# Dealing one block of the output projection unevenly over the DMA engines

## The chip, the cores and the metric

One core of a Trainium2 chip. The metric is device time in microseconds (us) of one execution of the kernel. Engines are named as in the profile: PE (TensorE matmuls), PEld (its weight loads), DVE (VectorE), ACT (ScalarE), POOL (GpSimd), SP (SyncE, whose queue issues nearly all transfers here). The core has 16 DMA engines, on which all transfers run.

## The reference, cut to what matters

```python
xn = layernorm(x)                              # x: [2, 1, 512]
q  = (xn @ wq)                                 # 32 heads of 128
k, v = caches[:, :, -4096:, :]                 # 8 kv heads, the last 4096 of 32768 positions
o  = softmax(q @ k.T / sqrt(128)) @ v          # each kv head serves 4 heads
s  = o.reshape(2, 1, 4096) @ wo                # wo: [4096, 512]
z  = gelu(xn @ w_in); z1, z2 = halves of z     # w_in: [512, 1792]
g  = silu((z1 * (w_sp * layernorm(z2) + b_sp)) @ w_out)
return x + s * g
```

All of it is fp32, two batch rows and one position. Nearly every byte that is read (wq, w_in, w_out, wo and the window of both caches, 89.4 MB together) is used once.

## The kernel before, in words

Everything large comes through one queue: SP issues the transfers in program order, `w_in`, `w_out`, `wq` in two halves, then one 4 MB load of k or v for each of the 8 kv heads (a "unit"), and `wo` last. All 4 MB loads, the halves of wq, `w_in` and the two parts of `wo` share a ring of four SBUF slots (`slot`), so that SP waits at most issues for the unit that last used the slot. SP also reuses eight landing semaphores in turn: an issue that gets a semaphore waits until the transfer that had it before has landed.

For each unit DVE turns k in four pieces (`turn`, tile `kt`), PE makes scores (`s`), DVE and ACT make probabilities (`sm`, `p`), PE and DVE bring them into shape (`pp`, `pT`), and PE multiplies them with v (`values`, tile `acc`). `collect` and `spread` gather the heads of a set of units into `oT`, the weights for the output projection. There are three sets (`SETS`): units 0 to 3 with 16 blocks of `wo`, units 4 and 5 with 8, units 6 and 7 with 8. A block is 128 rows of `wo`, one on each partition, and within a set row 16p + j (or 8p + j) belongs to partition p of block j.

The last part of the program multiplies `oT` with the blocks of `wo` as they land. The blocks of the sets 0 and 1 are added up in the PSUM tile `part`, each step on one of four column strips of PE; `wo_early` emits one landed piece of these. Then ACT copies `part` to `parts`, PE folds the four strips into `so` with `rowm`, and the blocks of set 2 are added to `so` directly, in pieces of 4, 2, 1 and 1 blocks, in the order in which they land. DVE multiplies `so` with the gate and adds x (`res`), and ACT issues the store.

`wo` is loaded in eight transfers, in this order: blocks 0 to 7 and 8 to 15 of set 0 (2 MB each), blocks 0 to 3 and 4 to 7 of set 1, and 4, 2, 1 and 1 blocks of set 2:

```python
for j, n in (((0, 8), (8, 8)), ((0, 4), (4, 4)), ((0, 4), (4, 2), (6, 1), (7, 1)))[i]:
    sp.dma_start(t[:, a : a + n, :], wo_s[i][:, j : j + n, :])
    blocks.append((t[:, a : a + n, :], sets[f"oT{i}"][1], j))
```

The helper `InOrder` records every operation of PE, DVE, ACT and SP, so that in the profile they all stand at its line 37; tiles tell them apart.

Of the kernel before, what the change touches and what calls it, by code (L numbers as in the profile page):

```python
# [9 lines left out]
F32 = mybir.dt.float32  # L10
# [4 lines left out]
P = 128  # L15
# [6 lines left out]
def free_ap(t, offset, dims):  # L22

    return bass.AP(tensor=t.tensor, offset=t.offset + offset, ap=[list(t.ap[0])] + [list(d) for d in dims])
# [18 lines left out]
def kernel(  # L43
# [13 lines left out]
    nc = tc.nc  # L57
    pe, dve, act, sp = (InOrder(tc, e) for e in (nc.tensor, nc.vector, nc.scalar, nc.sync))
    B, _, D = x.shape
    _, HKV, SK, _ = k_cache.shape  # L60
# [20 lines left out]
    cst = ctx.enter_context(tc.tile_pool(name="cst", bufs=1))  # L81
# [3 lines left out]
    def slot(name, *shape):  # L85
        return ring.tile([P, *shape], F32, tag="slot", name=name)

    def bank(name, *shape):
        return ps.tile([P, *shape], F32, tag="kt", name=name, bufs=3)
# [11 lines left out]
    for a in range(0, KT, 2):  # L101
        t = slot(f"wq{a}", 2, HQ * DH)
# [1 line left out]
        wqt += [t[:, 0], t[:, 1]]  # L104

    wb1 = cst.tile([1, 2], F32, tag="wb1", name="wb1")
    act.dma_start(wb1[:, 0:1], bass.AP(tensor=w_sp.tensor, offset=w_sp.offset, ap=[[1, 1], [1, 1]]))
    act.dma_start(wb1[:, 1:2], bass.AP(tensor=b_sp.tensor, offset=b_sp.offset, ap=[[1, 1], [1, 1]]))
    x4 = low.tile([P, DC], F32, tag="x4", name="x4")
    nc.gpsimd.memset(x4, 0.0)  # L110
    by_group = [[DC, G], [D, B], [1, DC]]
# [14 lines left out]
    def turn(p, c):  # L126
        t = sb.tile([P, CT, G, 32], F32, tag="kt", name=f"kt{p.n}_{c}", bufs=4)
        dve.transpose(t.rearrange("p t j y -> p (t j y)"), p.k[:, CT * c : CT * c + CT, :].rearrange("p t d -> p (t d)"))
        p.kt.append(t)

    units = []
    for n in range(HKV):
        p = Unit()
        p.n, p.kt, p.s = n, [], None
        units.append(p)
    AHEAD = 2
# [8 lines left out]
    ident = cst.tile([P, P], F32, tag="ident", name="ident")  # L145
# [8 lines left out]
    hT = low.tile([P, FT, 32], F32, tag="hT", name="hT")  # L154
    nc.gpsimd.memset(hT, 0.0)

    rowm = cst.tile([P, 32], F32, tag="rowm", name="rowm")
    dve.tensor_reduce(rowm, ident.rearrange("p (g c) -> p c g", g=G), axis=AX.X, op=ALU.add)

    def rsqrt(dst, a, tag):  # L160
        t = cst.tile(list(a.shape), F32, tag="rt" + tag, name="rt" + tag)
        act.activation(t, a, AF.Ln)
        act.activation(dst, t, AF.Exp, scale=-0.5)
        dve.tensor_mul(t, dst, dst)
        dve.tensor_mul(t, t, a)
        dve.tensor_scalar(t, t, -0.5, 1.5, op0=ALU.mult, op1=ALU.add)
        dve.tensor_mul(dst, dst, t)


    st = cst.tile([B, nc.vector.BN_STATS_DIM], F32, tag="st", name="st")  # L170
    dve.bn_stats(st, xs)
    mv = cst.tile([B, nc.vector.BN_AGGR_DIM], F32, tag="mv", name="mv")
    dve.bn_aggr(mv, st)
    va = cst.tile([B, 1], F32, tag="va", name="va")
    dve.tensor_scalar_add(va, mv[:, 1:2], EPS)
    rs = cst.tile([B, 1], F32, tag="rs", name="rs")
    rsqrt(rs, va, "x")
    xn = sb.tile([B, D], F32, tag="o", name="xn", bufs=1)
    dve.tensor_scalar(xn, xs, mv[:, 0:1], rs, op0=ALU.subtract, op1=ALU.mult)
    pt = bank("xnT_ps", KT, B)  # L180
# [26 lines left out]
    def place(n, nx):  # L207
        t = cst.tile([P, nx, n, REP, G, nx], F32, tag=f"place{n}", name=f"place{n}")
        nc.gpsimd.memset(t, 0.0)
        for x in range(nx):  # L210
            dve.tensor_add(
                t[:, x, :, :, :, x], *(free_ap(ident, REP * b, [[E, n], [1, REP], [32, G]]) for b in range(B))
            )
        return t
# [6 lines left out]
    for k in range(KT):  # L221
        for n in range(G):
# [3 lines left out]
                start=(k == 0), stop=(k == KT - 1),  # L226
# [14 lines left out]
    def queries(k):  # L241
        for r in range(NR):
            for g in range(G):
                c = (r * G + g) * 512
                pe.matmul(
                    pq[r][32 * g : 32 * g + 32, :], xnT[:, k, :], wqt[k][:, c : c + 512],
                    start=(k == 0), stop=(k == KT - 1),
                )
# [34 lines left out]
    dve.tensor_mul(hT[:, :, 0 : 16 * B : 16], z1, z2)  # L283
    queries(2)
    place4 = place(4, 2)
    place2 = place(2, 4)
    py = bank("ys", D)
    for j in range(FT):
# [17 lines left out]
    for r in range(NR):  # L306
        src = pq[r].rearrange("p (i d) -> p i d", i=REP)
# [5 lines left out]
    for r in range(NR):  # L313
        pt = bank(f"qT_ps{r}", REP, G, 32)
# [4 lines left out]
    for j in range(G):  # L319
        pe.matmul(  # L320
            pw[:, j, :], selj[:, j].rearrange("p g c -> p (g c)"), qT.rearrange("p r g b i -> p (r g b i)"),
            start=True, stop=True,
# [10 lines left out]
    sets = {}  # L333
    for i, (kv, n, nj) in enumerate(SETS):
        o1 = cst.tile([P, B, 32], F32, tag=f"o1_{i}", name=f"o1_{i}")
        lt = cst.tile([P, CH], F32, tag=f"lt_{i}", name=f"lt_{i}")
        nc.gpsimd.memset(lt, 1.0)
        oT = cst.tile([P, nj, 32], F32, tag=f"oT_{i}", name=f"oT_{i}")
# [5 lines left out]
    def scores(p, *chunks):  # L344
        if p.s is None:
            p.s = ps.tile([P, 512], F32, tag="s", name=f"s{p.n}", bufs=2)
        for j in range(G):
            for c in chunks:
                pe.matmul(
                    p.s[32 * c : 32 * c + 32, :], qw[:, p.n, j].rearrange("p g e -> p (g e)"), p.kt[c][:, :, j, :],  # L350
                    start=(j == 0), stop=(j == G - 1),
                )
# [93 lines left out]
    def spread(i):  # L446
        o1, oT, nj = sets[f"oT{i}"]
        t = {8: place2, 16: place4}[nj]
        nx = 32 // nj
        pt = bank(f"oT_ps{i}", B, nj)  # L450
        for x in range(nx):
            pe.matmul(
                pt, t[:, x].rearrange("p n h g x -> p (n h g x)"), o1[:, :, nj * x : nj * x + nj],
                start=(x == 0), stop=(x == nx - 1),
            )
        dve.tensor_copy(oT[:, :, 0 : 16 * B : 16], pt.rearrange("p b j -> p j b"))

    ends = {kv + n - 1: i for i, (kv, n, nj) in enumerate(SETS)}
    def gathered(p):
        if p is not None:  # L460
            collect(p)

    def spread_after(p):
        if p is not None and p.n in ends:
            spread(ends[p.n])

    def probabilities(p, between):
        row_max(p)
        share_max(p)
        between(0)  # L470
        bias(p)
        probs(p)
        swapped(p)
        between(1)
        probs_t(p)

    def product(p):
        if p is not None:
            values(p)
            evacuate(p)  # L480

    old = None
    for prev, cur in zip([None] + units, units):
        gathered(old)
        if prev is not None:
            probabilities(prev, lambda c: turn(cur, c))
        turn(cur, 2)
        spread_after(old)
        turn(cur, 3)
        old = prev if cur.n < HKV - AHEAD else units[-3] if cur.n == HKV - 1 else None  # L490
        product(old)
        scores(cur, 0, 1, 2, 3)


    wo_s = []
# [3 lines left out]
    blocks = []  # L499
    for first, of in ((0, (0,)), (1, (1, 2))):  # L500
        t = slot(f"wo{first}", 16, D)
        a = 0
        for i in of:
            nj = SETS[i][2]
            for j, n in (((0, 8), (8, 8)), ((0, 4), (4, 4)), ((0, 4), (4, 2), (6, 1), (7, 1)))[i]:
                sp.dma_start(t[:, a : a + n, :], wo_s[i][:, j : j + n, :])
                blocks.append((t[:, a : a + n, :], sets[f"oT{i}"][1], j))
                a += n
    EARLY = 24
    done = 0  # L510

    def wo_early(n):
        nonlocal done
        t, oT, j = blocks[n]
        for a in range(t.shape[1]):
            g = done % G
            pe.matmul(
                part[32 * g : 32 * g + 32, :], oT[:, j + a, :], t[:, a, :], start=(done < G), stop=(done >= EARLY - G)
            )
            done += 1  # L520
# [9 lines left out]
    wo_early(0)  # L530
    gathered(units[-1])
    spread_after(units[-1])
    for n in range(1, 4):
        wo_early(n)
    parts = sb.tile([P, D], F32, tag="o", name="parts", bufs=1)
    act.activation(parts, part, AF.Copy)
    so = bank("so", DC)
    for g in range(G):
        pe.matmul(so[32 * g : 32 * g + 32, :], rowm, parts[:, g * DC : (g + 1) * DC], start=True, stop=False)
    for n in range(4, len(blocks)):  # L540
        t, oT, j = blocks[n]
        for a in range(t.shape[1]):
            for g in range(G):
                pe.matmul(
                    so[32 * g : 32 * g + 32, :], oT[:, j + a, :], t[:, a, g * DC : (g + 1) * DC],
                    start=False, stop=(j + a == oT.shape[1] - 1),
                )
# [32 lines left out]
```

## Time and profile before

| what | us |
|---|---|
| time, median of 3 runs | 217.88 (217.22 to 217.9) |
| the profiled execution's own time | 217.06 |
| its span in the trace | 215.3 |
| the last piece of wo has landed, in the span | 211.47 |

| engine | busy us | share of the span |
|---|---|---|
| PE | 139.3 | 65% |
| PEld | 44.0 | 20% |
| DVE | 104.8 | 49% |
| ACT | 24.0 | 11% |
| POOL | 4.0 | 2% |

The profiled execution's time is 1.76 us more than its span, which is what lies around the program. The DMA engines moved 89.54 MB in the span, 416 GB/s on average. The page's row of 40 slices shows them at nine tenths or more from the second slice to the last but one.

### The profile page before, as it was taken

The numbers are of one execution on the slowest core, as the hardware profiler recorded it, in microseconds if no ns is written. First come the engines' busy times: TensorE is split into PE (matmuls) and PEld (weight loads), VectorE is DVE, ScalarE is ACT, GpSimd is POOL, SyncE is SP. The second block draws the span as 40 slices with busy tenths as digits, with TensorE's granted clock in tenths as the row PEclk, the third lists the DMA queues.
The fourth block names the chain that finished last, engine by engine and source line by source line (L and its number), as shares of the span: only waits on it lengthen the run. The fifth ranks groups of instructions, "written<-read, shape, count | busy, mean of one in ns | idle before, by whom it ended". The sixth has DMA issues, their size and how long they took to land.

```text
span 215.3 us, 2106 instructions
## 1 busy us (share of the span) xinstructions
PE 139.3 (65%) x862; PEld 44.0 (20%) x862; DVE 104.8 (49%) x161; ACT 24.0 (11%) x60; POOL 4.0 (2%) x20
## 2 busy tenths in 40 slices
PE   0174195827756973982595298089669299969773
PEld 0120021213111211220121022033111022332321
DVE  2604014159658559439506921983693883511201
ACT  5002103110001101011020002102010102021010
POOL 7000000000000000000000000000000000000000
PEclk9999557995596796697579669757967959988789
DMA  7999999999999999999999999999999999999990
GB/s 256 427 438 451 426 438 438 406 457 414 457 408 444 423 438 432 426 451 420 451 405 451 420 444 426 426 451 417 444 414 451 426 440 417 432 417 425 414 386 27
DMA packets 4093, 89.54 MB, mean 416 GB/s; under 512 B 486, under 2 KB 498, under 8 KB 884
## 3 DMA queue, kind: packets, MB, share of 16 engines
q1 hardware_dynamic: 4032, 89.39, 96.8%
q8 instruction: 7, 0.11, 0.2%
q14 instruction: 2, 0.02, 0.0%
q10 hardware_dynamic: 20, 0.01, 0.0%
q0 software_dynamic: 32, 0.00, 0.0%
HBM read 89.40 MB, written 0.00 MB: 415 GB/s over the span
## 4 chain that ended last, share of the span: by engine, by line
DMA 72%; PE 14%; DVE 11%; SPq 1%; ACT 1%; issue 1%; ACTq 0%; DVEq 0%
DMA v<-in_A_v_cache_dram 42%; DMA k<-in_A_k_cache_dram 20%; DMA wo<-in_A_wo_dram 9%; DVE kt L37 8%; PE acc L37 8%; PE s L37 4%; PE pp L37 2%; SPq L37 1%; ACT p L37 1%; DVE pT L37 1%; DVE sm L37 1%; DVE qw L37 1%; DVE res L37 0%; PE so L37 0%; DVE mg L37 0%
## 5 line engine op out<-in xcount | busy, mean ns | idle before, releaser
L37 DVE STREAM_TRANSPOSE kt<-k 128x2048 f32<-128x2048 f32 x32 | 72.5, 2285 | 2.2 <-DMA k<-in_A_k_cache_dram 2.2
L37 PE MATMUL acc<-v,pT 128*32 128x512 f32 x256 | 42.5, 822 | 12.5 <-DMA v<-in_A_v_cache_dram 11.7
L37 PE MATMUL s<-kt,qw 128*32 128x512 f32 x256 | 38.0, 637 | 3.5 <-DVE kt L37 2.9
L37 PE MATMUL pp<-p,swap 128*128 128x512 f32 x16 | 12.5, 871 | 21.2 <-ACT p L37 21.2
L37 DVE CUSTOM_DVE_ANT_1 sm<-s,own 128x512 f32<-128x512 f32 x8 | 5.5, 692 | 34.4 <-PE s L37 34.3
L37 PEld LDWEIGHTS acc<-v,pT 128*32 128x32 f32 x256 | 11.1, 155 | 43.2 <-issue 40.0
L37 PE MATMUL q_ps<-wq,xnT 128*32 128x512 f32 x64 | 11.4, 852 | 10.1 <-DMA wq<-in_A_wq_dram 10.1
L37 ACT ACTIVATE o<-acc,diag 128x128 f32<-128x128 f32 x30 | 8.7, 369 | 72.9 <-PE acc L37 72.5
L37 PEld LDWEIGHTS s<-kt,qw 128*32 128x32 f32 x256 | 9.1, 115 | 30.5 <-issue 19.9
L37 ACT ACTIVATE p<-sm,nb 128x512 f32<-128x512 f32 x8 | 5.8, 724 | 66.5 <-DVE nb L37 66.5
L37 PE MATMUL z<-win,xnT 128*32 128x448 f32 x32 | 6.1, 939 | 4.5 <-DMA win<-in_B_w_in_dram 4.5
L37 DVE STREAM_TRANSPOSE pT<-pp 128x512 f32<-128x512 f32 x8 | 5.7, 715 | 5.6 <-PE pp L37 5.5
L37 PE MATMUL col<-o,selw 128*32 128x128 f32 (+1 forms) x28 | 7.8, 468 | 0.0
L37 DVE TENSOR_TENSOR lsum<-pl,diag 128x4 f32<-128x4 f32 x3 | 0.5, 161 | 14.8 <-PE pl L37 14.8
L37 PEld LDWEIGHTS pp<-p,swap 128*128 128x128 f32 x16 | 3.0, 234 | 22.0 <-ACT p L37 22.0
L37 PE MATMUL part<-wo,oT 128*32 128x512 f32 x48 | 7.4, 751 | 0.1
L37 PE MATMUL mo<-mg,same 128*128 128x16 f32 x16 | 3.2, 273 | 5.8 <-DVE mg L37 5.3
L37 ACT ACT_TABLE_LOAD x4 | 5.1, 1283 | 1.9 <-issue 1.9
L37 DVE STREAM_TRANSPOSE zt<-z 128x448 f32<-128x448 f32 x1 | 1.0, 980 | 8.9 <-ACT z L37 8.9
L37 PEld LDWEIGHTS q_ps<-wq,xnT 128*32 128x32 f32 x64 | 2.2, 142 | 14.7 <-DMA wq<-in_A_wq_dram 10.3
L37 PE MATMUL xnT_ps<-ident,xn 2*128 2x2 f32 x4 | 0.6, 252 | 6.9 <-DVE xn L37 6.9
L37 DVE TENSOR_TENSOR res<-so,gate 128x128 f32<-128x128 f32 x1 | 0.3, 292 | 9.6 <-PE so L37 9.6
(110 smaller groups left out, 66.3 us busy)
## 6 DMA issues: line engine op xcount, KB each, us to landing
k<-in_A_k_cache_dram SPq DMA_DIRECT2D x8, 4096.0 KB, 23.9
v<-in_A_v_cache_dram SPq DMA_DIRECT2D x8, 4096.0 KB, 31.4
wq<-in_A_wq_dram SPq DMA_DIRECT2D x2, 4096.0 KB, 28.8
wo<-in_A_wo_dram SPq DMA_DIRECT2D x2, 2048.0 KB
win<-in_B_w_in_dram SPq DMA_DIRECT2D x1, 3584.0 KB, 11.2
wo<-in_A_wo_dram SPq DMA_DIRECT2D x3, 1024.0 KB, 23.9
wout<-in_B_w_out_dram SPq DMA_DIRECT2D x1, 1792.0 KB, 15.1
wo<-in_A_wo_dram SPq DMA_DIRECT2D x1, 512.0 KB, 28.0
```

What stands on the lines that cost most here:

```text
L37: return self.tc.keep_in_program_order(call(*args, **kwargs))
```

## The change

The 16th block (block 15) of set 0 no longer comes with the blocks 8 to 14. Its 128 rows come in two transfers of their own:

- 80 rows go to partitions 0 to 79. The source is given in two dimensions, 10 by 8: place 8a + b takes row a + 10b.
- 48 rows go to partitions 16 to 63 of a new tile `wob`, whose partitions 0 to 15 are zero. The source is 8 by 6: place 6a + b takes row 80 + a + 8b.

Rows of block 15 thereby sit on other partitions than their weights in `oT`. So two matrices of zeros and ones (`perm`, written once by POOL and DVE) and a new function `deal` bring the weights of block 15 into the same order (`oTx`): two small matmuls and two small copies, in the iteration of unit 6. In the last part the block is two steps in place of one, of 80 and 64 rows, so `part` has 25 steps (`EARLY`).

Beside that, the two loads of single numbers (`w_sp`, `b_sp`) are issued by POOL in place of ACT, and four small tiles of the first layernorm share one.

```diff
-    act.dma_start(wb1[:, 0:1], ...w_sp...)
-    act.dma_start(wb1[:, 1:2], ...b_sp...)
+    nc.gpsimd.dma_start(wb1[:, 0:1], ...w_sp...)
+    nc.gpsimd.dma_start(wb1[:, 1:2], ...b_sp...)
...
+    NA, NBK = 80, 64
+    MA, MB = 10, 8
+    perm = cst.tile([P, NA + NBK], F32, tag="perm", name="perm")
+    nc.gpsimd.memset(perm, 0.0)
+    oTx = cst.tile([P, 2, 32], F32, tag="oTx", name="oTx")
+    nc.gpsimd.memset(oTx, 0.0)
+    wob = cst.tile([P, D], F32, tag="wob", name="wob")
+    nc.gpsimd.memset(wob[0:NBK, :], 0.0)
+    NX = P - NA
+    X0 = NBK - NX
...
+    dve.tensor_copy(
+        perm[:, 0:NA].rearrange("p (e i) -> p e i", e=MA), free_ap(ident, 0, [[1, MA], [MA, NA // MA]])
+    )
+    dve.tensor_copy(
+        perm[:, NA + X0 :].rearrange("p (e i) -> p e i", e=MB), free_ap(ident, NA, [[1, MB], [MB, NX // MB]])
+    )
...
+    def deal():
+        o1, oT, nj = sets["oT0"]
+        pt = bank("oTx_ps", 2, B)
+        for i, rows in ((0, slice(0, NA)), (1, slice(NA, NA + NBK))):
+            n = rows.stop - rows.start
+            pe.matmul(pt[0:n, i, :], perm[:, rows], oT[:, nj - 1, 0 : 16 * B : 16], start=True, stop=True)
+        for i, n in ((0, NA), (1, NBK)):
+            dve.tensor_copy(oTx[0:n, i, 0 : 16 * B : 16], pt[0:n, i, :])
...
         spread_after(old)
+        if cur.n == HKV - AHEAD:
+            deal()
         turn(cur, 3)
...
-            for j, n in (((0, 8), (8, 8)), ((0, 4), (4, 4)), ((0, 4), (4, 2), (6, 1), (7, 1)))[i]:
+            for j, n in (((0, 8), (8, 7)), ((0, 4), (4, 4)), ((0, 4), (4, 2), (6, 1), (7, 1)))[i]:
...
+            if i == 0:
+                for dst, p0, k, n in ((t[0:NA, a, :], 0, MA, NA // MA), (wob[X0:NBK, :], NA, MB, NX // MB)):
+                    src = wo_s[0][p0 : p0 + 1, nj - 1, :]
+                    row = nj * D
+                    sp.dma_start(
+                        dst, bass.AP(tensor=src.tensor, offset=src.offset, ap=[[row, k], [row * k, n], [1, D]])
+                    )
+                blocks.append((t[0:NA, a : a + 1, :], oTx[0:NA], 0))
+                blocks.append((wob[0:NBK, :].rearrange("p (a d) -> p a d", a=1), oTx[0:NBK], 1))
-    EARLY = 24
+    EARLY = 25
...
-    for n in range(1, 4):
+    for n in range(1, 6):
         wo_early(n)
...
-    for n in range(4, len(blocks)):
+    for n in range(6, len(blocks)):
```

On SP, at the end of its program, before (`wo_802` holds set 0, `wo_805` the sets 1 and 2; the sizes are partitions by elements, `DMAHW` are the landing semaphores):

```order
L37 DMA wo_802<-in_A_wo_dram 128x4096 [waits DMAHW3_49,DVE_49]
L37 DMA wo_802<-in_A_wo_dram 128x4096
L37 DMA wo_805<-in_A_wo_dram 128x2048 [waits DMAHW4_49,PE_49]
L37 DMA wo_805<-in_A_wo_dram 128x2048 x2
L37 DMA wo_805<-in_A_wo_dram 128x1024
L37 DMA wo_805<-in_A_wo_dram 128x512 [waits DMAHW5_49]
L37 DMA wo_805<-in_A_wo_dram 128x512 [waits DMAHW6_49]
```

The same place with the change (`wo_812` and `wob` hold set 0, `wo_817` the sets 1 and 2):

```order
L37 DMA wo_812<-in_A_wo_dram 128x4096 [waits DMAHW1_49,DVE_49]
L37 DMA wo_812<-in_A_wo_dram 128x3584
L37 DMA wo_812<-in_A_wo_dram 80x1x512
L37 DMA wob<-in_A_wo_dram 48x1x512 [waits Pool_49]
L37 DMA wo_817<-in_A_wo_dram 128x2048 [waits DMAHW2_49,PE_49]
L37 DMA wo_817<-in_A_wo_dram 128x2048
L37 DMA wo_817<-in_A_wo_dram 128x2048 [waits DMAHW3_49]
L37 DMA wo_817<-in_A_wo_dram 128x1024 [waits DMAHW4_49]
L37 DMA wo_817<-in_A_wo_dram 128x512 [waits DMAHW5_49]
L37 DMA wo_817<-in_A_wo_dram 128x512 [waits DMAHW6_49]
```

Two transfers stand between the second piece of set 0 and set 1. The turn of the eight semaphores has moved: the last two issues had waited for the loads of v of the units 6 and 7, and now wait for the first two pieces of `wo` itself, while the two issues ahead of them wait for those v loads.

On PE, in the last part, what comes after the heads of units 6 and 7 are spread, before:

```order
L37 MATMUL part<-wo_802,oT_333 32x512 x8
L37 MATMUL part<-wo_805,oT_338 32x512 x8
L37 MATMUL so<-parts,rowm 32x128 x4
L37 MATMUL so<-wo_805,oT_343 32x128 x32
```

And with the change:

```order
L37 MATMUL part<-wo_812,oT_338 32x512 x7
L37 MATMUL part<-wo_812,oTx 32x512
L37 MATMUL part<-wob,oTx 32x512
L37 MATMUL part<-wo_817,oT_343 32x512 x8
L37 MATMUL so<-parts,rowm 32x128 x4
L37 MATMUL so<-wo_817,oT_348 32x128 x32
```

One step more stands ahead of the steps of set 1 (17 in place of 16).

More of the change, by code (lines that the diff above doesn't have):

```diff
@@ L106 @@
     wb1 = cst.tile([1, 2], F32, tag="wb1", name="wb1")
-    act.dma_start(wb1[:, 0:1], bass.AP(tensor=w_sp.tensor, offset=w_sp.offset, ap=[[1, 1], [1, 1]]))
-    act.dma_start(wb1[:, 1:2], bass.AP(tensor=b_sp.tensor, offset=b_sp.offset, ap=[[1, 1], [1, 1]]))
+    nc.gpsimd.dma_start(wb1[:, 0:1], bass.AP(tensor=w_sp.tensor, offset=w_sp.offset, ap=[[1, 1], [1, 1]]))
+    nc.gpsimd.dma_start(wb1[:, 1:2], bass.AP(tensor=b_sp.tensor, offset=b_sp.offset, ap=[[1, 1], [1, 1]]))
     x4 = low.tile([P, DC], F32, tag="x4", name="x4")
@@ L167, in rsqrt @@
         dve.tensor_mul(dst, dst, t)
-    st = cst.tile([B, nc.vector.BN_STATS_DIM], F32, tag="st", name="st")
+    NS, NM = nc.vector.BN_STATS_DIM, nc.vector.BN_AGGR_DIM
+    sv = cst.tile([B, NS + NM + 2], F32, tag="sv", name="sv")
+    st, mv = sv[:, 0:NS], sv[:, NS : NS + NM]
+    va, rs = sv[:, NS + NM : NS + NM + 1], sv[:, NS + NM + 1 : NS + NM + 2]
     dve.bn_stats(st, xs)
-    mv = cst.tile([B, nc.vector.BN_AGGR_DIM], F32, tag="mv", name="mv")
     dve.bn_aggr(mv, st)
-    va = cst.tile([B, 1], F32, tag="va", name="va")
     dve.tensor_scalar_add(va, mv[:, 1:2], EPS)
-    rs = cst.tile([B, 1], F32, tag="rs", name="rs")
     rsqrt(rs, va, "x")
```

## The prediction

> **What bounds the kernel now.** I read the page first, its chain of work (part 4) and its DMA queues (part 3), then the chain in order of time for the end of the span.
>
> ```profile
> DMA 72%; PE 14%; DVE 11%; SPq 1%; ACT 1%; issue 1%; ACTq 0%; DVEq 0%
> q1 hardware_dynamic: 4032, 89.39, 96.8%
> q8 instruction: 7, 0.11, 0.2%
> ...
> 191.87 19.59 DMA wo<-in_A_wo_dram
> 211.47 0.04 issue
> 211.51 0.47 PE so L37 x8
> 211.98 0.02 issue
> 212.00 0.30 DVE res L37
> ```
>
> The chain is transfers for 72% of its length, and SP's queue (q1) keeps the sixteen DMA engines busy for 96.8% of the span. The span ends 3.8 us after the last piece of `wo` has landed at 211.47: one piece's matmuls, two DVE operations and the store. So the time is the landing of the last piece plus a constant, and the question is what the last landing waits for. Is the queue ever empty before the end? The tile view of v and the DMA view of 30 to 209 us:
>
> ```profile
> DMA to landing us min/median/max: 25.0/31.4/33.3
> ...
> DMA packets 3351, 77.03 MB, mean 430 GB/s; under 512 B 372, under 2 KB 372, under 8 KB 601
> q1 hardware_dynamic: 3343, 76.92, 99.8%
> q8 instruction: 6, 0.10, 0.2%
> q14 instruction: 2, 0.02, 0.0%
> ```
>
> Over these 179 us the engines are full. A load of v is 4 MB, 9.8 us at 430 GB/s, and lands 25.0 us after its issue at the earliest: at least 15 us of other work stand ahead of it. In the same stretch eight more packets come in between, from the queues that bring instructions: six of 16 KB (q8) and two of 8 KB (q14). Now the end, cut finely (the columns are PE, PEld, DVE, ACT, POOL, then granted clock, DMA share, GB/s):
>
> ```profile
> 208.40:208.80 0.40, 0.34 (x8) 0.07 (x8) 0.00 (x0) 0.00 (x0) 0.00 (x0) 1.00 1.00 394
> 208.80:209.20 0.40, 0.08 (x4) 0.11 (x8) 0.00 (x0) 0.00 (x0) 0.00 (x0) 1.00 0.89 353
> 209.20:209.60 0.40, 0.40 (x20) 0.40 (x23) 0.00 (x0) 0.00 (x0) 0.00 (x0) 1.00 0.62 241
> 209.60:210.00 0.40, 0.40 (x24) 0.33 (x12) 0.00 (x0) 0.00 (x0) 0.00 (x0) 1.00 0.48 184
> 210.00:210.40 0.40, 0.34 (x14) 0.14 (x9) 0.00 (x0) 0.00 (x0) 0.00 (x0) 1.00 0.40 154
> 210.40:210.60 0.20, 0.20 (x12) 0.20 (x11) 0.00 (x0) 0.00 (x0) 0.00 (x0) 1.00 0.32 123
> 210.60:210.80 0.20, 0.20 (x12) 0.03 (x4) 0.00 (x0) 0.00 (x0) 0.00 (x0) 1.00 0.17 62
> 210.80:211.00 0.20, 0.20 (x8) 0.13 (x8) 0.00 (x0) 0.00 (x0) 0.00 (x0) 1.00 0.08 31
> 211.00:211.20 0.20, 0.20 (x8) 0.03 (x4) 0.00 (x0) 0.00 (x0) 0.00 (x0) 1.00 0.06 20
> ```
>
> The share falls in two steps. Between 208.8 and 210.0 it drops from 1.00 to 0.40, which is 6.4 of 16 engines: about ten are done. Those left run on until 210.4 to 211.2. All have had the same bytes of the kernel, so six are late by something else, and six is the number of the 16 KB instruction packets. The middle of the first fall is near 209.3, of the second near 210.7: a late engine is 1.4 us behind. The packet records under this view, chained end to start, say the same: sixteen chains of 252 packets of q1, of which six have a 16 KB instruction packet among them. Those six end last, at 210.5 to 211.2; two with an 8 KB packet end at 209.9 and 210.0, the other eight at 208.9 to 209.6.
>
> **The dealing.** Block 15 is 128 rows of 2 KB. Before, each engine moved eight of them, 16 KB. One engine moves 430/16 = 26.9 GB/s, so 16 KB are 0.61 us. I assume that a transfer is dealt over as many engines as its outer count says, starting from the same one: 10 engines with eight rows each, then 8 of these with six more. No view numbers the engines, so two things are taken on trust here: that the deal goes this way, and that the six left out are the six late ones. What speaks for it is that the counts fit: 6 engines without rows, 2 with eight, 8 with fourteen, against 6, 2 and 8 chains that end late, a little late and early. [...]
>
> What a single 2 KB row costs comes from the last piece, eight rows of 2 KB per engine; PE's loads of the last pieces are these:
>
> ```profile
> 202.00 5.60 PE L37 MATMUL part<-wo,oT 128*32 128x512 f32 x32
> 206.53 0.16 PEld L37 LDWEIGHTS part<-wo,oT 128*32 128x32 f32 x8 [1.05 <-DMA wo<-in_A_wo_dram]
> 207.66 0.60 ACT L37 ACTIVATE parts<-part 128x512 f32<-128x512 f32 x1 [8.99 <-PE part L37]
> 208.31 0.16 PEld L37 LDWEIGHTS so<-parts,rowm 128*32 128x32 f32 x8 [1.62 <-ACT parts L37]
> 209.12 2.18 PE L37 MATMUL so<-wo,oT 128*32 128x128 f32 x56 [0.38 <-DMA wo<-in_A_wo_dram]
> 210.87 0.16 PEld L37 LDWEIGHTS so<-wo,oT 128*32 128x32 f32 x8 [0.24 <-DMA wo<-in_A_wo_dram]
> 211.51 0.16 PEld L37 LDWEIGHTS so<-wo,oT 128*32 128x32 f32 x8 [0.48 <-DMA wo<-in_A_wo_dram]
> ```
>
> The last two pieces land 0.64 us apart, 0.08 us a row. So an engine with fourteen rows needs 1.12 us for block 15 in place of 0.61, 0.51 more; one with eight 0.03 more; one with none 0.61 less. The last late engine goes from 211.2 to 210.6. The last early one goes from about 209.6 to 210.1, and the two with the 8 KB packet stay at 210.0, or come to 210.5 if they are among the eight. All remain below 210.6. **The gain is 0.6 us**, and it is also the ceiling: nothing in the change relieves an engine of more. How much of it comes through depends on which engine starts late in a given execution, so I allow 0.3 to 0.65.
>
> **Can the end use it?** PE must be there when the pieces land. The steps of `part` begin at 202.00, after the heads of the last two units are spread, which the change does not touch. In this stretch the clock is half:
>
> ```profile
> 202.00:205.60 3.60, 3.60 (x21) 1.01 (x24) 0.18 (x1) 0.00 (x0) 0.00 (x0) 0.53 1.01 426
> ```
>
> The 24 matmuls ahead of the last eight (set 1's second piece) were done about 206.1, and the last eight waited for their piece until 206.53. With one step more (two matmuls, some 0.2 to 0.4 us) PE is done with those at 206.3 to 206.5, while the piece now lands about 205.9. So the last eight begin where they began, or 0.2 earlier, and `so` begins with set 2 at 208.8 at the latest, since 208.31 and the fold's half microsecond stay. The four-block piece lands 0.6 earlier, at 208.4; its matmuls waited 0.38 before, and now are late by up to 0.4. They take about 0.8, ending at 209.6, when the next piece lands. From there PE waits for every piece as before, and the 0.6 reaches the end.
>
> **The rest of the change** costs nothing on that path. `deal` puts two small matmuls behind `pp` on PE and two small copies on DVE between two turns of k, under a turn of 2.3 us, so the copies find their input ready; they delay the issue of the v load that waits for that turn:
>
> ```profile
> 192.02 0.18 DVE L37 COPY oT<-oT_ps 128x16 f32<-128x16 f32 x1
> ...
> 159.03 4.40 DVE kt L37 x2
> ...
> 163.45 28.41 DMA v<-in_A_v_cache_dram
> ```
>
> Two copies of 0.18 make 0.4 us, against 28.4 from issue to landing, of which 9.8 is the transfer itself: more than 15 us of queue cover it. Were that cover gone, 0.4 would be lost. SP's two extra issues and its new waits lie likewise ahead of need: the last issue now waits for the second piece of `wo`, which lands near 201, and is wanted near 209. At the start POOL issues two more loads ahead of the identity matrix:
>
> ```profile
> 1.29 0.68 POOL L112 DMA_DIRECT2D x<-in_A_x_dram  x1 [0.21 <-POOL ident masks.py:197]
> 2.40 0.37 DVE L37 TENSOR_REDUCE rowm<-ident 128x32 f32<-128x128 f32 x1 [2.40 <-POOL ident masks.py:199]
> 12.06 6.08 PE L37 MATMUL z<-win,xnT 128*32 128x448 f32 x32 [4.52 <-DMA win<-in_B_w_in_dram]
> 18.06 0.38 PE L37 MATMUL wb_ps<-wb,ones 1*128 1x2 f32 x2
> ```
>
> Two issues of 0.68 are 1.4 us for the identity and the layernorm behind it, and PE stood idle for 4.52 before `z` until w_in had landed. The two numbers are read at 18.06. If that cover were gone, the delay would still fall into the queue's 15 us.
>
> So the profiled execution would go from 217.06 to 216.5. The median lies 0.8 above it, from late starts or lags that the change leaves, and goes from 217.88 to **217.3**, 0.27% less. About 0.3% is what a measurement of this kernel can tell from no change, so the forecast lies close to that line.
>
> **Rivals.**
>
> *The rows crowd each other (no gain).* Before, each engine has written its own share of partitions; the new transfers send ten engines to partitions 0 to 79 and eight to 16 to 63. If two engines that write into the same stretch of SBUF go at half speed, eight rows cost 1.28 in place of 0.64, and the loaded engines end at 210.1 + 0.64 = 210.7, those with the 8 KB packet at 211.1. That takes away 0.1 to 0.5 of the gain, say 217.7. [...]
>
> *The deal misses (no gain, or a little loss).* If rows are dealt over all sixteen engines, every engine has eight 2 KB rows in place of part of a longer one, 0.03 more: 217.9. If it goes over ten, but a late engine is among the loaded, the last landing is 0.51 later: 218.4.
>
> *One more instruction packet (slower).* The seventh 16 KB packet of q8 came at the very end, when nothing was left to delay:
>
> ```profile
> DMA packets 4, 0.02 MB, mean 20 GB/s; under 512 B 1, under 2 KB 1, under 8 KB 3
> q8 instruction: 1, 0.02, 5.5%
> ```
>
> That is the window of 211 to 212. PE's program grows by three matmuls, six in the trace's count (each stands there twice), with as many weight loads. If the packet comes that much earlier, within the last pieces, and on a loaded engine that still has rows, this engine ends 1.4 us after its 210.1 to 210.6: at 211.5 to 212.0, later than before by up to 0.8 us, 218.6. It decides once the packet comes before 210.6. Six matmuls are less than one piece's eight, and I expect it after 210.5, so this is not likely.
>
> **How the numbers follow.** Forecast (0.6 us gained) 0.64; crowding 0.13; a miss 0.10; one more packet, or a half-clock stretch that falls on PE's last steps, 0.13. The range goes from 216.5, below the forecast by the spread of the runs shown, to 218.5, which takes in the crowding, the miss and most of the slower rival. The forecast's own range is 216.9 to 217.6. Its 0.64 lie on both sides of the 0.3% line; I give 0.46 to faster, since the six and ten fit so well that the full 0.6 is likelier than a part, and 0.18 to the same. Crowding and most of a miss add 0.19 to the same, the rest is slower.
>
> **What would show it.** In the changed kernel's trace the DMA share should fall from 1.00 to below 0.2 in about 1.3 us, with no step at 0.4, and the last `so` loads should start near 210.9. If the share has its step still, with the end at 211.2 or later, the deal missed; if rows of the two new transfers take twice 0.08, it is crowding; if q8 shows seven packets before the last landing, it is the instruction packet. If the last `so` loads wait for PE rather than for `wo`, my account of the end is wrong.

## The result, and the profile after

The changed kernel takes 219.45 us, the median of 9 runs (218.29 to 220.44), where the kernel before took 217.88 (216.86 to 218.08) beside it. The ratio is 1.0084, with a 95% interval of 1.0056 to 1.0112: slower by 0.8%. The profiled execution took 219.24, with a span of 217.1 (before 217.06 and 215.3). So 0.4 of its 2.2 us more lie outside the span: over the nine runs the time is 2.15 above the span on average, where it was 1.76 above it in the profiled execution before. What makes this part is open.

The page of the changed kernel: the same bytes in 146 packets more, and the queue as full as before. Of the 146, 128 are the rows of block 15 and 18 are packets of 4 bytes. Before, q1 has 448 of these for 28 transfers, one per engine and transfer; 18 more are the ten and eight engines of the new deal.

```profile
q1 hardware_dynamic: 4178, 89.39, 96.6%
DMA packets 4299, 89.54 MB, mean 412 GB/s; under 512 B 564, under 2 KB 576, under 8 KB 1090
DMA 59%; DVE 18%; PE 16%; SPq 3%; ACT 2%; issue 1%; ACTq 0%; DVEq 0%
```

The end of the chain in order of time, and from the tile view the issues of `wo`:

```profile
184.01 26.08 DMA wo<-in_A_wo_dram
210.09 0.14 issue
210.22 3.57 PE so L37 x64
213.79 0.02 issue
213.82 0.30 DVE res L37
```

```profile
L37 SPq DMA_DIRECT2D wo<-in_A_wo_dram x9: 327/376/965, 179.9 to 201.7; - x9
DMA to landing us min/median/max: 10.8/20.5/26.1
```

Two things have changed. The last issue, at 201.7, landed 10.8 us later, at 212.5, where the last piece had landed at 211.47. And PE no longer waits for the last pieces: its 64 matmuls into `so` ran 3.57 us without a stop and ended at 213.79, 0.8 later than 212.5 plus the 0.47 that the last eight took before. 1.05 of landing and 0.8 of PE are the 1.8 by which the span grew.

Where did the transfers lose a microsecond? Stretches of 1 us, first of before, then of after (columns as before: PE, PEld, DVE, ACT, POOL, granted clock, DMA share, GB/s):

```profile
199.00:200.00 1.00, 0.85 (x14) 0.46 (x10) 0.17 (x2) 0.00 (x0) 0.00 (x0) 1.00 0.85 360
200.00:201.00 1.00, 0.00 (x0) 0.00 (x0) 0.85 (x5) 0.00 (x0) 0.00 (x0) 1.00 0.98 418
201.00:202.00 1.00, 0.99 (x8) 0.97 (x9) 0.00 (x0) 0.00 (x0) 0.00 (x0) 1.00 1.03 434
202.00:203.00 1.00, 1.00 (x9) 0.37 (x12) 0.18 (x1) 0.00 (x0) 0.00 (x0) 0.60 0.97 410
```

```profile
199.00:200.00 1.00, 0.06 (x1) 0.00 (x0) 0.80 (x5) 0.00 (x0) 0.00 (x0) 1.00 1.16 346
200.00:201.00 1.00, 0.78 (x7) 0.78 (x8) 0.16 (x1) 0.00 (x0) 0.00 (x0) 1.00 0.91 205
201.00:202.00 1.00, 0.53 (x7) 0.34 (x10) 0.18 (x1) 0.00 (x0) 0.00 (x0) 1.00 1.12 350
202.00:203.00 1.00, 1.00 (x12) 0.31 (x8) 0.00 (x0) 0.00 (x0) 0.00 (x0) 1.00 0.85 311
```

The engines are as busy as before, and move 1.21 MB in these 4 us in place of 1.62: 0.41 MB, at 430 GB/s 0.95 us. The packet records tell what that is. From 199.4 to 202.7, while the rows of block 15 are written, packets take longer on all sixteen chains: the 14 KB ones up to 0.96 us (0.535 elsewhere), the 8 KB ones up to 0.70 (0.309), the 2 KB ones up to 0.23 (0.084). Chains that carry no row of block 15 lose the same microsecond with their packets of other transfers. Below, a kernel "stretches" if it shows this.

The chains also show the deal, and where the 16 KB instruction packets (q8) fell. The end of each of the sixteen chains, with the number of its 2 KB rows of block 15 (where several packets start within a few ns, they were told apart by the order of sizes that each engine must have):

```
14 rows  210.84 210.86 211.06 211.28 211.30 211.60 211.75   and 212.20 (the one with a 16 KB packet)
 8 rows  210.46 210.78
 0 rows  211.07 211.13 211.15 211.31 211.42 (each with a 16 KB packet)   and 209.86 (without one)
```

Eight chains have 14 rows, two 8, six none, as forecast. But only five of the six late engines are among the six without rows. The sixth packet fell on a loaded engine, and this one ends last.

### The profile page after: what moved, and what is told of

It is laid out like the page before. It is cut to its first block, busy times and chain, and to the rows that moved or that the text cites. A ratio compares the mean times of both kernels' runs of the same rounds, so it can differ in the third digit from the quotient of the medians.

```text
span 217.1 us, 2128 instructions
## 1 busy us (share of the span) xinstructions
PE 137.1 (63%) x868; PEld 45.6 (21%) x868; DVE 105.3 (48%) x165; ACT 24.0 (11%) x60; POOL 5.9 (3%) x25
## 4 chain that ended last, share of the span: by engine, by line
DMA 59%; DVE 18%; PE 16%; SPq 3%; ACT 2%; issue 1%; ACTq 0%; DVEq 0%
DMA k<-in_A_k_cache_dram 33%; DVE kt L37 14%; DMA v<-in_A_v_cache_dram 14%; DMA wo<-in_A_wo_dram 12%; PE s L37 6%; PE acc L37 5%; PE pp L37 4%; SPq L37 3%; PE so L37 2%; ACT p L37 2%; DVE pT L37 1%; DVE sm L37 1%; DVE qw L37 1%; DVE mg L37 0%; DVE res L37 0%
## 5 line engine op out<-in xcount | busy, mean ns | idle before, releaser
L37 PE MATMUL acc<-v,pT 128*32 128x512 f32 x256 | 39.0, 764 | 11.4 <-DMA v<-in_A_v_cache_dram 10.5
L37 PE MATMUL s<-kt,qw 128*32 128x512 f32 x256 | 40.2, 656 | 3.8 <-DVE kt L37 2.7
L37 PE MATMUL pp<-p,swap 128*128 128x512 f32 x16 | 13.1, 912 | 21.6 <-ACT p L37 21.6
L37 PEld LDWEIGHTS acc<-v,pT 128*32 128x32 f32 x256 | 10.4, 150 | 39.2 <-issue 34.3
L37 PE MATMUL q_ps<-wq,xnT 128*32 128x512 f32 x64 | 10.6, 796 | 12.1 <-DMA wq<-in_A_wq_dram 12.1
L37 PEld LDWEIGHTS s<-kt,qw 128*32 128x32 f32 x256 | 10.0, 118 | 31.2 <-issue 18.1
L37 PE MATMUL part<-wo,oT 128*32 128x512 f32 x46 | 6.0, 601 | 3.0 <-DMA wo<-in_A_wo_dram 3.0
L37 PE MATMUL z<-win,xnT 128*32 128x448 f32 x32 | 4.8, 765 | 3.1 <-DMA win<-in_B_w_in_dram 3.1
L37 PEld LDWEIGHTS mo<-mg,same 128*128 128x128 f32 x16 | 2.4, 188 | 11.8 <-DVE mg L37 11.8
```

The lines of the kernel that those rows point to most:

```text
L37: return self.tc.keep_in_program_order(call(*args, **kwargs))
```

## Experiments

In the table, each kernel has the last column from its own windows; the kernel before has 418 there, the changed one 205. Two theories stood against each other: **stretching** (the way block 15's rows are written slows the transfers, whichever engine carries them), and **the wrong six** (rows and instruction packets meet on one engine). Three things could make the stretching: the order in which the source is read, engines that write into the same partitions, or engines that write other partitions than the ones they have in a plain transfer (the place theory). The expectations call the first the source or order theory and the second the write theory. No trace names the engine or the partition of a packet, so the last two can be told only by what a deal costs. The kernel before ran beside each group: 217.68 beside e1 to e4, 217.37 beside e5 to e8, 217.35 beside e9 to e11; the ratios are to these.

| kernel | median us (runs) | ratio to before, 95% | GB/s from 200 to 201 us |
|---|---|---|---|
| e1, block plain, two half steps | 217.56 (12) | 0.9999 [0.998, 1.0018] | 410 |
| e2, loads as before, the rest changed | 217.56 (12) | 1.002 [0.9993, 1.0047] | 410 |
| e3, 80 and 48 rows over 16 engines each | 219.9 (6) | 1.009 [1.0055, 1.0124] | 223 |
| e4, single numbers back on ACT | 219.66 (6) | 1.0089 [1.006, 1.0118] | 231 |
| e5, 80 and 48 rows, source in plain order | 218.91 (4) | 1.0064 [1.0039, 1.0089] | 260 |
| e6, 10 by 8 and 8 by 6, each partition once | 219.18 (6) | 1.0079 [1.005, 1.0108] | 287 |
| e7, one transfer of 128, source 16 by 8 | 218.41 (10) | 1.0053 [1.003, 1.0075] | 231 |
| e8, plain 80 and 48, each partition once | 219.22 (4) | 1.0084 [1.0052, 1.0115] | 270 |
| e9, four of 32 rows, 8 by 4 | 218.37 (11) | 1.0071 [1.0047, 1.0096] | 430 |
| e10, the same four, 16 by 2 | 219.68 (6) | 1.0099 [1.0077, 1.012] | 254 |
| e11, e9 with the numbers on POOL | 218.98 (6) | 1.0084 [1.0051, 1.0116] | 420 |

**e1.** Block 15 as one plain transfer, used in two steps of half the partitions; all else as changed.

```diff
-                for dst, p0, k, n in (...): sp.dma_start(dst, ...10 by 8, 8 by 6...)
+                sp.dma_start(t[:, a : a + 1, :], wo_s[0][:, nj - 1 : nj, :])
+                blocks.append((t[0:64, 15:16, :], sets["oT0"][1][0:64], 15))
+                blocks.append((t[64:P, 15:16, :], sets["oT0"][1][64:P], 15))
```

> The changed kernel with block 15 as one plain transfer of 128 rows of 2 KB, one row a partition, in place of the two dealt ones; its two steps of part take partitions 0 to 63 and 64 to 127. All else as changed, deal included (its result is unused). Source theory (2 KB rows that stand 32 KB apart in wo crowd the memory): packets of 14, 8 and 2 KB stretch as in the changed kernel, to 0.9, 0.4 to 0.6 and 0.12 to 0.2 us, between 199 and 203 us, and the time is 218.7 to 219.3. Write theory (several engines write into one stretch of partitions): no packet stretches, every engine keeps its eight rows, the time is that of the kernel before plus at most 0.3, 217.7 to 218.2.

Its stretch of 200 to 201:

```profile
200.00:201.00 1.00, 0.29 (x2) 0.20 (x2) 0.60 (x4) 0.00 (x0) 0.00 (x0) 1.00 0.99 410
```

410 GB/s, 2 KB rows of 84 ns: rows of 2 KB from the same source addresses stretch nothing. What is lost hangs on how they are dealt and placed.

**e2.** `wo` loaded as before, block 15 in two half steps; all else as changed.

```diff
-            for j, n in (((0, 8), (8, 7)), ...): sp.dma_start(t[:, a : a + n, :], ...)   # and the two dealt transfers
+            m = 8 if n == 7 else n
+            sp.dma_start(t[:, a : a + m, :], wo_s[i][:, j : j + m, :])
```

> As the run before, but block 15 comes with the blocks 8 to 14 in one transfer of 2 MB, as in the kernel before: every DMA of wo is the old one, while deal, the extra step of part, the added tiles and the loads from POOL stay. Both DMA theories: 217.7 to 218.0, no change against before. If the step on PE, deal or POOL's loads are the cost, it stays at 219 or more.

217.56: `deal`, the step more on PE and POOL's loads together cost nothing that can be measured. The part outside the span is there too, 2.15 us on average against 1.85 in the runs of before beside it, and the span is as much shorter (medians 215.4 and 215.7).

**e3.** Sixteen engines with five rows and sixteen with three, on the same partitions.

```diff
-    MA, MB = 10, 8
+    MA, MB = 16, 16
```

> The changed kernel with the same 80 and 48 rows on the same partitions, but with the source dealt 16 by 5 and 16 by 3, so that all sixteen engines take 8 rows in all. Source theory: the packets stretch as in the changed kernel, time 219 to 219.5 (nothing relieved, nothing loaded). Write theory: the same partitions are written, by more engines at once, so packets stretch too, 219 to 219.5. If it is the uneven dealing itself that costs (a loaded engine that is also late), the time is 218.0.

```profile
200.00:201.00 1.00, 0.88 (x8) 0.88 (x8) 0.07 (x1) 0.00 (x0) 0.00 (x0) 1.00 0.84 223
```

No engine has more rows than another, and it stretches just the same. The uneven count is not the cause. Here no engine is relieved or loaded, and the last packet of `wo` ends at 212.19, against 211.19 before and 212.20 in the changed kernel: 1.0 us is the price of the stretch alone.

**e4.** The single numbers issued by ACT, as before.

```diff
-    nc.gpsimd.dma_start(wb1[:, 0:1], ...)   # and wb1[:, 1:2]
+    act.dma_start(wb1[:, 0:1], ...)         # and wb1[:, 1:2]
```

> The changed kernel with the loads of the two single numbers issued by ACT again, as before. If moving them to POOL had turned the engines that bring PE's instructions by one, so that one of the six packets fell on an engine with fourteen rows, all six now fall on engines without rows, the end is 0.5 to 0.9 earlier and the time 218.6 to 218.9. If not, 219.4 as changed, with one loaded engine last.

One of its windows and the end of its chain:

```profile
200.00:201.00 1.00, 0.70 (x7) 0.70 (x7) 0.24 (x1) 0.00 (x0) 0.00 (x0) 1.00 0.95 231
...
201.97 10.57 DMA wo<-in_A_wo_dram
212.58 0.47 PE so L37 x8
```

Here PE waits for the last piece again, so the landing alone sets the end: 212.5, 1.1 after before's, as in the changed kernel. The six 16 KB packets fell on five engines without rows and on one with eight, which ended last; one engine without rows got none and was done at 209.91. With the loads back on ACT, a packet still fell on an engine with rows.

**e5.** Source in plain order, on the same partitions.

```diff
-    MA, MB = 10, 8
+    MA, MB = 1, 1
```

> The changed kernel with the same 80 rows on partitions 0 to 79 and 48 on 16 to 63, but in plain order: place p takes row p, or row 80 + p. Write theory (partitions 0 to 79 and 16 to 63 take what all 128 took before): the packets stretch as in the changed kernel, time 219.0 to 219.8. Order theory (the source taken with strides of 8 and 10 rows is what slows): no stretch, 217.5 to 218.0.

```profile
200.00:201.00 1.00, 0.68 (x6) 0.69 (x7) 0.26 (x1) 0.00 (x0) 0.00 (x0) 1.00 0.94 260
```

It stretches; the order of the source is not the cause. This deal too goes over all sixteen engines, five rows and three: q1 has 160 packets more than before, the 128 rows and twice 16 of 4 bytes.

**e6.** The changed deal, but with 80 rows on partitions 48 to 127 and 48 on 0 to 47, so that no partition is written twice, and one step on PE.

```diff
+    dealt(t[48:128, a, :], 0, 10, 8)
+    dealt(t[0:48, a, :], 80, 8, 6)
```

> The same uneven dealing, 10 by 8 and 8 by 6, but into all 128 partitions of the old tile, each written once: 80 rows on 48 to 127, 48 rows on 0 to 47, one step of part. Write theory: little or no stretch, the six late engines keep their 0.6, and this is the version that gains, 217.0 to 217.4. Order theory: it stretches as changed, 219.

```profile
200.00:201.00 1.00, 1.00 (x16) 0.24 (x8) 0.35 (x1) 0.58 (x2) 0.00 (x0) 1.00 0.99 287
```

**e7.** One transfer to all 128 partitions, only its source dealt.

```diff
+    dealt(t[0:128, a, :], 0, 16, 8)
```

> Block 15 as one transfer into all 128 partitions of the old tile, but with the source dealt 16 by 8 (place 8a + b takes row a + 16b): eight rows an engine. Write theory: every partition is written once, so no stretch, or a short one where two engines meet, 217.6 to 218.0. Order theory: it stretches as changed, 219 to 219.8.

```profile
200.00:201.00 1.00, 1.00 (x16) 0.26 (x12) 0.17 (x1) 0.37 (x1) 0.00 (x0) 1.00 0.90 231
```

**e8.** Both transfers with plain source, on partitions 0 to 79 and 80 to 127.

```diff
+    dealt(t[0:80, a, :], 0, 1, 80)
+    dealt(t[80:128, a, :], 80, 1, 48)
```

> Block 15 as two transfers in plain order, 80 rows on partitions 0 to 79 and 48 on 80 to 127 of the old tile. Beside the run with the same split on 0 to 79 and 16 to 63 this changes the second range alone. Write theory: 217.6 to 218.0. If it is the split in two transfers with fewer than 128 partitions that costs, whatever they write: 219.

```profile
200.00:201.00 1.00, 0.50 (x5) 0.50 (x5) 0.41 (x2) 0.00 (x0) 0.00 (x0) 1.00 0.91 270
```

All three write every partition once, and all three stretch: 287, 231 and 270 GB/s. So it is not that partitions 16 to 63 get two transfers' rows. e6, from which the write theory expected 217.0 to 217.4, took 219.18; e7's 218.41 lies between its two expectations. The transfer of e7 reaches every partition, as e1's does, and runs at 231 GB/s against 410: the reach of the partitions does not tell them apart.

**e9.** What is left is which engine writes which partition. Four transfers of 32 rows, dealt 8 by 4, to partitions 0 to 31 and 32 to 63 of the old tile and of `wob`, so that eight engines carry 16 rows each and eight none (q1 has 32 packets of 4 bytes more than before, four times eight); the numbers on ACT.

```diff
+    for m in range(4):
+        dst = (t[:, a, :], wob)[m // 2][32 * (m % 2) : 32 * (m % 2) + 32, :]
+        ...  # source rows 32m to 32m + 31, 8 by 4
```

> [...] The two numbers are loaded by ACT, as before. Place theory: packets keep 0.084 and 0.309, the late engines are relieved, the last landing is 0.4 to 0.6 earlier than in the kernel before: 216.9 to 217.3. Rival (every dealt transfer of fewer than 128 rows costs, wherever it writes): it stretches, 218.5 to 219.5.

```profile
200.00:201.00 1.00, 0.01 (x1) 0.01 (x1) 0.83 (x5) 0.00 (x0) 0.00 (x0) 1.00 1.04 430
201.00:202.00 1.00, 1.00 (x8) 1.00 (x8) 0.00 (x0) 0.00 (x0) 0.00 (x0) 0.82 0.98 416
```

No stretch at all: 430 and 416 GB/s. The place theory has it so if these eight engines write only partitions that they have in a plain transfer; that they do was the author's assumption, and no trace shows it.

The chains show what the deal itself brings without stretching:

```
16 rows  209.81 209.86 209.90 210.32 210.48 210.71 210.91   and 211.21 (16 KB packet)
 0 rows  209.93 209.96 209.98 210.09 210.18 (16 KB packet)   and 208.55 208.86 209.22 (without)
```

The relieved late engines end at 210.2 at the latest, 1.0 before the 211.2 of before. But again one packet of the six fell on a loaded engine, and the last piece lands at 211.54, where it landed before. Were that packet on a relieved engine, the last chain would end at 210.91, 0.3 earlier. So the 216.9 to 217.3 that was expected did not come, though the packets kept their times: the median is 218.37.

**e10.** The same four transfers to the same partitions, dealt 16 by 2. By the place theory this stretches again, 218.5 to 219.5.

```diff
-    ap=[[row, 8], [row * 8, 4], [1, D]]
+    ap=[[row, 16], [row * 16, 2], [1, D]]
```

> The same four transfers of 32 rows onto the same partitions, but dealt 16 by 2: all sixteen engines take two rows of each, eight in all. [...] Rival: the same time as the run before.

```profile
200.00:201.00 1.00, 0.68 (x6) 0.68 (x7) 0.26 (x1) 0.00 (x0) 0.00 (x0) 1.00 0.81 254
202.00:203.00 1.00, 0.64 (x4) 0.20 (x8) 0.00 (x0) 0.00 (x0) 0.00 (x0) 0.70 0.75 176
```

254 against 430 GB/s with the same partitions, the same source rows and as many transfers of the same size. What differs is which engine takes which rows to which partitions, with sixteen engines and two rows each in place of eight with four (64 packets of 4 bytes more than before, in place of 32). So "small transfers stretch" falls. The place theory foretold both runs, but that the engines keep to places of their own in e9 and leave them in e10 was not shown. Nor is it separated why a deal costs: by that theory an engine at the place of another could be the cause by itself, and so could two engines that meet there.

**e11.** e9 with the single numbers on POOL, as in the change.

> The 8 by 4 dealing with the two numbers loaded by POOL, as in the changed kernel. If the loads from POOL turn the engines that bring PE's instructions by two, so that the sixth packet falls on one of the eight loaded engines, this engine ends last: 217.7 to 218.2, 0.5 to 0.9 more than with ACT. If not, the same as with ACT.

```profile
200.00:201.00 1.00, 0.49 (x5) 0.49 (x5) 0.42 (x2) 0.00 (x0) 0.00 (x0) 1.00 1.01 420
...
201.99 10.16 DMA wo<-in_A_wo_dram
212.19 0.47 PE so L37 x8
```

No stretch again (the window's row). In the chain's rows the last piece lands at 212.15, not earlier: a loaded engine had a 16 KB packet and ended at 211.82, the other fifteen at 211.01 or before. The packets follow each other over the engines in one fixed order, if a duration tells an engine (..., 879, 935, 931, 922, 960, 960, 948, 879, ... ns), and kernels start at different points of it: the kernel before, e1, e4, e5, e8 and e10 at 935, the changed kernel, e3, e7 and e9 at about 930, e2, e6 and e11 at 879. Where the numbers are issued does not sort them.

**e12.** e9's times fall into two groups, 217.63 to 218.37 and 219.57 to 220.07. Three more profiled executions of the same program, the second to the fourth, and a second one of the changed kernel, ask whether the packets' turn or the clock makes them.

> A second look at the 8 by 4 dealing onto own places, with ACT loading the two numbers: the same program, another execution. Turning theory (the engines that bring PE's instructions are not the same in every execution): the first of the six 16 KB packets takes another engine than in the first look, or the same by chance, and the last landing follows from it: near 211.5 to 212.1 if a loaded engine has one, 210.9 to 211.2 if none has. Clock theory (a half-clock stretch on PE's last matmuls makes the slow group of times near 219.6 to 220.1): a look that takes 219.5 or more shows the half clock between 208 and 213 and the last landing no later than the others.

> A third look at the same program. Turning theory: last landing near 211.5 to 212.1 if a loaded engine has one of the six packets, 210.9 to 211.2 if none has. Clock theory: a time of 219.5 or more comes with the half clock on the last matmuls.

> A fourth look at the same program. Turning theory: last landing near 211.5 to 212.1 if a loaded engine has one of the six packets, 210.9 to 211.2 if none has. Clock theory: a time of 219.5 or more comes with the half clock on the last matmuls.

> A second look at the changed kernel. Turning theory: the six packets need not fall as in the first look, where one fell on an engine with fourteen rows; the stretch of packets between 199 and 203 is the same in any case.

The three took 219.77, 218.9 and 217.71; the changed kernel 220.19. The packets stood at the same point of their order in each execution of a program (four of e9, two of the changed kernel). So this point belongs to the program, and does not turn between executions. The clock is what differs. First the second execution, windows and the end of its chain, then the fourth:

```profile
204.30:208.70 4.40, 4.40 (x18) 0.59 (x16) 0.00 (x0) 0.00 (x0) 0.00 (x0) 0.50 0.98 410
208.70:211.00 2.30, 2.30 (x16) 0.20 (x4) 0.00 (x0) 0.00 (x0) 0.00 (x0) 0.50 0.57 221
...
211.33 0.61 ACT parts L37
211.98 2.22 PE so L37 x72
```

```profile
204.30:208.70 4.40, 3.83 (x26) 0.60 (x20) 0.00 (x0) 0.50 (x1) 0.00 (x0) 0.88 1.00 417
208.70:211.00 2.30, 2.08 (x56) 1.38 (x56) 0.00 (x0) 0.09 (x1) 0.00 (x0) 1.00 0.56 218
...
201.53 10.08 DMA wo<-in_A_wo_dram
211.66 0.47 PE so L37 x8
```

The transfers run alike, 410 and 417 GB/s, 221 and 218. In the second execution PE has half the clock for 6.83 us (204.27 to 211.09), is at the steps of `part` until 211, and runs all of `so` behind the last landing. In the fourth the half clock lasts 3.41 us and ends at 205.35, ahead of them. That is 2 us of time: 219.77 against 217.71. The third was like the second (`so` without a wait from 211.00). The second execution of the changed kernel stretches like the first, and again PE ends it:

```profile
200.00:201.00 1.00, 0.72 (x7) 0.72 (x7) 0.22 (x1) 0.00 (x0) 0.00 (x0) 1.00 0.97 209
...
210.74 4.00 PE so L37 x72
```

No kernel of these beat the one before; e1 and e2 equal it.

## Why the prediction was wrong, point by point

The step that failed is the sum that ends in "All remain below 210.6". The chains of the changed kernel end at 209.86 to 212.20, for two reasons: about 1.0 us of stretching on every engine, which the sum did not have, and an instruction packet on a loaded engine. Then PE added 0.8 behind the last landing.

- **The end is the last landing plus a constant**: right of the kernel before and of e4, wrong of the changed kernel. The step "can the end use it?" put the half clock where the trace of before had it, at 202 to 205.6, and gave a stretch on PE's last steps only a part of a 0.13. In the changed kernel it lay here:

```profile
209.60:210.00 0.40, 0.31 (x8) 0.04 (x6) 0.00 (x0) 0.00 (x0) 0.00 (x0) 1.00 1.02 405
210.00:210.40 0.40, 0.18 (x4) 0.21 (x8) 0.00 (x0) 0.00 (x0) 0.00 (x0) 0.61 0.93 364
210.40:210.80 0.40, 0.40 (x12) 0.40 (x11) 0.00 (x0) 0.00 (x0) 0.00 (x0) 0.50 0.92 353
210.80:211.20 0.40, 0.40 (x16) 0.40 (x11) 0.00 (x0) 0.00 (x0) 0.00 (x0) 0.50 0.64 246
211.20:211.60 0.40, 0.40 (x16) 0.40 (x12) 0.00 (x0) 0.00 (x0) 0.00 (x0) 0.50 0.24 92
211.60:212.00 0.40, 0.40 (x16) 0.40 (x12) 0.00 (x0) 0.00 (x0) 0.00 (x0) 0.50 0.08 31
```

  The clock is half from 210.09 to 213.50, PE is busy throughout, and the 0.8 us behind the last landing are its price. The last `so` matmuls wait for PE, which the prediction had named as the sign that its account of the end is wrong. The traces show what goes ahead of it: from 206.68 to 210.09 PE was busy for 1.49 of 3.41 us, since the second piece of set 1 came late and PE stood idle for 1.37 until it had landed. In e4, the same kernel but for two small loads, PE was busy for 2.06 of the 3.41 us from 207.33, and the clock stayed full to the end of the matmuls. So late pieces may bring the late half clock about; no run tests it, and it would not explain e9, whose pieces are not late. Times above 219 us, where such a stretch is likely but was not seen in each, are none of 65 of the kernel before in these comparisons, 1 of 12 of e1, 2 of 12 of e2 and 5 of 11 of e9. Why stays open.
- **The deal**: right. Ten and eight engines, shown by the 18 packets of 4 bytes and by the 14, 8 and 0 rows of the chains. The share of the engines does fall without a step at 0.4 (the rows above, 0.92 to 0.08 in 1.2 us), as forecast; but the last piece lands at 212.5 and not near 210.9, so the shape of the fall alone proves no gain.
- **The six left out are the six late ones**: wrong, one of the two things taken on trust. Counts that fit were no evidence: in the changed kernel, e4, e6, e9 and e11 one or more of the packets fell on engines with rows. It is the rival "the deal misses" in its second form, and near its price of 0.5: in e11, which does not stretch, the loaded engine with a packet ended 0.8 after all others, and the last piece landed 0.7 later than in the kernel before (212.15 against 211.47).
- **What a row costs**: 0.08 us was right where nothing stretches (e1, e9: 0.084). In the deal of the change it was up to 0.23.
- **"The rows crowd each other"** named the right rows with the wrong reach and price. It held that only loaded engines pay, 0.64 each, and came to 217.7. That two engines in one stretch of SBUF go at half speed was its assumption, and no run shows it. On that assumption itself the price was too small: it doubled eight of the fourteen rows, and all fourteen at half speed are 1.12 more, which takes the whole gain. The runs show about 1.0 us on every engine, those without rows too, and also where every partition is written once (e6 to e8). This is the mis-sized term that turned the sign. The ends add up with it: a loaded engine without a packet was early, 208.9 to 209.6 before; with 0.51 for its rows, 1.0 for the stretching and 1.4 for a packet it comes to 211.8 to 212.5, and ended at 212.20. A relieved one with a packet goes from 210.5 to 211.2 by -0.61 and 1.0 to 210.9 to 211.6; they ended at 211.07 to 211.42.
- **The rest of the change costs nothing**: right as a whole, by e2. `deal`'s copies stand at 161.2, POOL's loads leave `z` where it was:

```profile
L37 DVE COPY oTx<-oTx_ps x2: 116/126/137, 161.2 to 161.3; 80x2 f32<-80x2 f32 x1, 64x2 f32<-64x2 f32 x1
...
12.23 4.82 PE L37 MATMUL z<-win,xnT 128*32 128x448 f32 x32 [3.10 <-DMA win<-in_B_w_in_dram]
16.98 0.38 PE L37 MATMUL wb_ps<-wb,ones 1*128 1x2 f32 x2
```

- **One more instruction packet before the end**: did not happen; six came before the last landing, as before.

So the 0.6 us hoped for was lost to the packet that fell on a loaded engine: the last packet ends where e3's does, which relieves no engine. The stretching put the landing about 1.0 later than before, and in the profiled execution the late half clock cost 0.8 more. That the stretching hangs on which engine takes which rows to which partitions is shown by e9 against e10 (430 and 254 GB/s). Where the packets wait was not shown.

## What to carry to other kernels

When a transfer is dealt by hand over the DMA engines, measure the deal beside the plain transfer and beside another deal onto the same partitions (32 rows 8 by 4 kept 430 GB/s, 16 by 2 got 254), and read packet durations on all engines, not only on the loaded ones: here a quarter of a megabyte, dealt over sixteen engines in e3, held the end of the transfers up by a microsecond (212.19 against 211.19). Before work is moved off engines that look late, find out what makes them late and whether it hits the same engines in the program as changed; a matching count is not a matching set. And an end that waits for transfers in one profile can be PE's in the next, if a half-clock stretch of 3.4 us may fall on its last steps.

## What the runs showed of the hardware

- One 256 KB block, dealt over the DMA engines in seven ways (the changed kernel, e3, e5 to e8, e10), slowed the transfers to 176 to 287 GB/s in single microseconds, against 410 to 430 with the block plain (before, e1, e2) or dealt 8 by 4 onto partitions 0 to 31 and 32 to 63 (e9, e11). In the changed kernel packets took longer on all sixteen engines, rows of 2 KB up to 0.23 us for 0.084.
- Instructions come in 16 KB packets (q8), six before the last landing, of 0.88 to 0.97 us while the queue is full, each in the chain of one DMA engine. That they are PE's is the author's estimate from the numbers of instructions: 868 matmuls and 868 weight loads, the next engine 165. Their durations follow each other in one order, whose start differs between programs but was the same in four executions of one; if a duration tells an engine, they go over the engines in this order. What sets the start is open.
- The same program ran its last steps at full or half clock from one execution to the next, with 3.41 or 6.83 us of half clock, worth 2 us (217.71 and 219.77). In the traces before and after the change each fall to half clock between 20 and 212 us followed 3.41 us in which PE was busy for at most 66%; not every such stretch was followed by one.
